# Attention with product-key experts on one core: three groups of tokens gathered and one dense, in place of two and two, with slots paced by counted VectorE work

## The chip, the core and the metric

One core of a Trainium2 chip runs the kernel. Its engines work in order, each from its own queue, and wait for each other by semaphores: TensorE (PE in the profile, PEld for its weight loads), VectorE (DVE), ScalarE (ACT), GpSimd (POOL, which here only starts gathers after the beginning) and SyncE (SP, which issues nearly all other transfers, in order). The metric is the device time of one execution in microseconds, the median of three runs.

## The reference, cut to what matters

```python
xn = layernorm(x)                       # x: 2048 tokens, 512 wide
out = x + A(xn) + B(xn)

# A: 32 query heads of 16, one key and one value head
p = softmax((xn @ wq) @ k.T * 16 ** -0.5);  A = (p @ v) @ wo

# B: 32 heads; per head two scores of 64 keys, the best two of each
s1, s2 = q1 @ k1.T, q2 @ k2.T           # q = xn @ w_q
cand = t1[:, None] + t2[None, :]        # 4 sums of the best 2 and 2
top_s, top_e = the best 2 of the 4      # top_e = i1 * 64 + i2, of 4096 experts
g = softmax(top_s)
act = gelu(xn . u[top_e])
B = sum over heads and the two of g * act * v[top_e]
```

So each token has 32 x 2 = 64 experts out of 4096, each a row of `u` (512) and a row of `v` (512).

## The kernel before

**Staging.** The 2048 tokens are 16 tiles of 128, in four groups of 512 (`GT` = 4 tiles). A prologue normalises and transposes the groups, projects queries, keys and values, and stores what is needed later in DRAM. Then a loop of 256 steps (and 24 more to run out) carries three streams, and its order of instructions on each engine is written out by hand (a manual schedule): what the program emits first, an engine does first.

- *Attention* (`att_steps`): 32 units (a block of 512 queries and four heads each) of 16 key tiles; a step does two key tiles. TensorE makes scores (L317), ScalarE exponentials (L320), TensorE the sums over values (L331). Behind each unit its sums are copied out (L339). From step 72 on, every 64 steps, `block_out` multiplies four tiles of a finished query block by `wo`.
- *Scores of the experts* (`score_thread`, a generator that gives the cost of each piece in units of about a microsecond of TensorE): for each chunk `c` of four heads (`NC` = 8) the weight is formed once (`wp_make`), for each tile of the group an `item` does twelve matmuls (L531) and VectorE finds the best of eight sets of 64 keys (L541, L543); after four tiles `batch` turns them into indices and gates. `run_scores` lets the thread run in each step until its spent cost reaches `aim`, which grows evenly to `FILL` at step 256.
- *The experts themselves*, in one of two ways. For a **gathered** group each of a token's 64 experts is a slot: GpSimd gathers the 128 rows of `uv` (1024 wide, 512 KB) for one tile (`gather`, L842), VectorE takes the product with the tokens (`dot`, L854), three small operations (`CHAIN`) and ScalarE's tanh (L870) give a weight for four slots at a time (`weigh`, L877), and VectorE adds the weighted row of `v` to the tile's total (`add`, L889). For a **dense** group (`dense`), 32 one-hot products (L713 to L716, L729) spread the gates over all 4096 experts into DRAM (`d_g`); then 32 blocks of 128 experts are computed whole: `pact` (L781), the activation on ScalarE and VectorE, and `pout` (L764), whose sums VectorE adds to the totals (L767). Rows of `ub` and `vb` are split in two parts by ScalarE (L677) and VectorE (L678).

**Order around the change.** In a step, `mid` emits the tanh of the groups of four that are complete, then this step's products (`todo` of them), then `go` emits adds, one at a time between the small operations and what is left of a dense block, and after them up to four gathers. At the step's end `fill` runs the score thread. A gather is emitted only while fewer than 12 (`NGB`) slots are between gather and add, and two fewer while `lent` is 2: `load_wo` borrows two of the gather buffers, from the step where `i` is 124 (modulo 128; `i` is twice the step) until 30, and near the end. Adds take slots whose tanh was emitted, so not before the step behind their product.

The products per step come from `pos`: 2.4 while group 0 is scored, then 1.9, 2.3 or 1.5 by what the thread does (`dense_on`), and in the last quarter evenly what is left. The groups are scored in the order of `SEQ`: 0, two chunks of 1, 2 (then its dense work), the rest of 1, 3 (then its dense work). Groups 0 and 1 are gathered (`NSP` = 2).

A tile's total holds the residual and the experts' part. The attention part is joined through DRAM: whichever of the two is ready first is stored to `d_part` and read back into `fin` when the other comes (`block_out`, `experts_out`, `load_fin`), and the sum is stored.

Of the kernel before, what the change touches and what calls it, by code (L numbers as in the profile page):

```python
# [10 lines left out]
F32 = mybir.dt.float32  # L11
# [11 lines left out]
P = 128  # L23
S = 2048
D = 512
# [27 lines left out]
@with_exitstack  # L53
def tile_kernel(ctx, tc, x, wq, wkv, wo, wqT, kT, uv, ub, vb, out):
    nc = tc.nc
    pool = lambda name, **kw: ctx.enter_context(tc.tile_pool(name=name, **kw))
    dram = pool("dram", bufs=1, space=DRAM)
    const = pool("const", bufs=1)
    big = pool("big", bufs=1)
    late = [None]  # L60
# [18 lines left out]
    d_part = [dram.tile([P, D], F32, name=f"dpart{t}") for t in range(NT)]  # L79


    ident = const.tile([P, P], F32, name="ident")
# [40 lines left out]
    XT, XN, ACC, XP = {}, {}, {}, [None]  # L123
# [256 lines left out]
        nc.vector.tensor_mul(on, OT.pop(pp), rs)  # L380
        ON[pp] = on

    DONE_A, DONE_B, OUTS = {}, {}, []
    WO, lent = [], [0]

    def load_wo():
# [25 lines left out]

    PL = []

    FIN = {}

    def load_fin(t):
        fin = late[0].tile([P, D], F32, name="fin", tag="fin", bufs=1)
        nc.sync.dma_start(fin, d_part[t])
        FIN[t] = fin  # L420

    def block_out(qb, j):
        t = 4 * qb + j
        p = xtile("pwo")
        for k in range(KC):
            nc.tensor.matmul(p, ON[4 * qb + k][:, j * P:(j + 1) * P], WO[k // 2][:, k % 2, :],  # L426
                             start=k == 0, stop=k == KC - 1)
        if t in FIN:
            fin = FIN.pop(t)

            def total():
                nc.vector.tensor_add(fin, fin, p)
                store(lambda: nc.sync.dma_start(out[t * P:(t + 1) * P, :], fin))

            behind(total)
        else:
            def keep():
                fin = late[0].tile([P, D], F32, name="fin", tag="fin", bufs=1)
                nc.scalar.copy(fin, p)
                store(lambda: nc.sync.dma_start(d_part[t], fin))  # L440

            on_act(keep)
        DONE_A[t] = True

    def experts_out(t):

        if t >= 12:
            return True
        if t in FIN:
            fin = FIN.pop(t)  # L450
            nc.vector.tensor_add(fin, fin, ACC[t])
            store(lambda: nc.sync.dma_start(out[t * P:(t + 1) * P, :], fin))
        elif t in DONE_A:
            load_fin(t)
            return False
        else:
            acc = ACC[t]
            store(lambda: nc.sync.dma_start(d_part[t], acc))
        DONE_B[t] = True
        return True  # L460


    WC = {}
# [12 lines left out]
    def wp_make(c):  # L476

        wt = [big.tile([P, 2, 512], F32, name="wt", tag="da", bufs=2) for _ in range(2)]
        for h in range(4):
            for n in range(4 * c + h + 1, min(4 * c + h + 3, 4 * NC) if late[0] else 4):  # L480
                if ("raw", n // 4, n % 4) not in WC:
                    wp_load(n // 4, n % 4)
            w = WC.pop(("raw", c, h))
            p = xtile("pw")
            for s in range(2):
                nc.tensor.matmul(p[s * E:(s + 1) * E, :], kTs[:, s, :], w[:, s, :], start=True, stop=True)
            nc.scalar.copy(wt[h // 2][:, h % 2, :], p)
            yield 0.9
        WC[c] = []
        for k in range(KC):  # L490
            p = xtile("pwt")
            for h in range(4):
                nc.tensor.transpose(p[:, h * P:(h + 1) * P], wt[h // 2][:, h % 2, k * P:(k + 1) * P], ident)
            wk = wk_tile()
            nc.vector.tensor_copy(wk[:, 0, :], p)
            nc.vector.tensor_tensor(out=wk[:, 1, :], in0=p, in1=wk[:, 0, :], op=OP.subtract)  # L496
            WC[c].append(wk)
            store(lambda k=k, wk=wk: nc.sync.dma_start(d_w[c][:, k], raw(wk[:])))
            yield 0.45

    def wp_read(n, ks=range(KC)):
        for k in ks:
# [1 line left out]
            nc.sync.dma_start(raw(wk[:]), d_w[SEQ[n][1]][:, k])  # L504
            WC.setdefault(n, []).append(wk)

    SEQ = ([(0, c) for c in range(NC)] + [(1, c) for c in range(2)] + [(2, c) for c in range(NC)]
           + [(1, c) for c in range(2, NC)] + [(3, c) for c in range(NC)])
    M8, I8 = {}, {}
    BT = 4  # L510

    def item(n_, ti):
        ph, c = SEQ[n_]
        nph, nc_ = SEQ[n_ + 1] if n_ + 1 < len(SEQ) else (None, None)
        t = TPH * ph + ti
# [24 lines left out]
        for s in range(8):  # L540
            nc.vector.max(m8[:, jb, s, :], p[:, s * E:(s + 1) * E])  # L541
# [102 lines left out]
    def dense(DG, after):  # L644
# [64 lines left out]
        def onehot(q):  # L709
            if q < NQ:  # L710
                tb = q * TB
                oa = kt(F16, (P, P, TB))
                nc.vector.tensor_tensor(out=oa, in0=io, in1=bc(0, tb, P), op=OP.is_equal)  # L713
                ob = kt(F16, (P, NB, TB))
                nc.vector.tensor_tensor(out=ob, in0=io[:, :NB, :], in1=bc(1, tb, NB), op=OP.is_equal)
                nc.vector.tensor_mul(ob, ob, bc(2, tb, NB))  # L716
                OH[q] = oa, ob

        onehot(0)
        onehot(1)  # L720
        for q in range(NQ):
# [5 lines left out]
            p = xtile("pg")  # L727
# [45 lines left out]
        for b in range(NB):  # L773
# [47 lines left out]
        yield from sums()  # L821
        if after is not None:
            wp_read(after, range(2, KC))
        OUTS.extend(range(GT * DG, GT * DG + GT))

# [5 lines left out]
    NSL = len(slots)  # L831
# [48 lines left out]
    def add(m):  # L880
        ph, c, ti, s = slots[m]
        n, i = divmod(m, SB)
        weigh(n)
        if i == SB - 1:
            weigh(n + 1)
        w = WT[n]
        acc = ACC[TPH * ph + ti]
        v = UV.pop(m)[:, D:]
        nc.vector.scalar_tensor_tensor(acc, v, w[:, i:i + 1], acc, op0=OP.mult, op1=OP.add)  # L889
        if c == NC - 1 and s == NEG - 1:  # L890
            OUTS.append(TPH * ph + ti)


    g_next, d_next, a_next, a_ready = [0], [0], [0], [0]
# [72 lines left out]
                yield from dense(ph, n + 1 if n + 1 < len(SEQ) else None)  # L967
                dense_on[0] = 0

    dense_on = [0]  # L970
    sgen = score_thread()
    spent = [0.0]

# [19 lines left out]
    def att_steps(d, mid, fill):  # L993
# [4 lines left out]
        if out_now and 4 * qb + j in DONE_B:  # L998
            load_fin(4 * qb + j)
        if i < STEPS:  # L1000
            u, kc = divmod(i, 16)
            if i == 0:
# [97 lines left out]
    with tc.manual_schedule(engines={E_.PE, E_.Activation, E_.DVE, E_.Pool, E_.SP}):  # L1100
        done0 = spent[0]
        half = STEPS // 2
        pos = 0.0
        for d in range(half + 24):


            if d < half * 3 // 4:
                pos += 2.4 if len(IDX) < NC * TPH else (1.9, 2.3, 1.5)[dense_on[0]]
            else:
                pos += max(0.0, NSL - pos) / max(half - 4 - d, 1)  # L1110

            todo = min(int(pos + 0.001), NSL) - d_next[0]

            def mid():
                post = POST[:]
# [51 lines left out]
        while a_next[0] < NSL:  # L1167
# [3 lines left out]
            adds(SB)  # L1171
            run(STORES)
            gathers(NGB)
        assert not OUTS
        run(STORES)


# [35 lines left out]
```

## Time and profile before

| | us |
|---|---|
| median of 3 runs (2034.71 to 2038.64) | 2036.56 |
| the profiled execution | 2035.25 |
| its span, first to last instruction | 2033.5 |
| TensorE busy in it | 1889.3 |
| VectorE busy | 1742.0 |
| ScalarE busy | 1245.1 |
| GpSimd busy | 585.9 |
| mean granted TensorE clock | 0.959 |

The profile is one execution. A group of instructions is named by engine and source line, with what it writes and reads; busy time is the union of its instructions, and instructions of one engine overlap at their ends, so the mean duration of one is longer than the distance from its start to the next one's. A wait is given to the instruction that ended it. Times in a timeline are microseconds from the span's start.

### The profile page before, as it was taken

What the parts mean: (1) busy time and instruction counts of PE and PEld (TensorE: products, weight loads), DVE (VectorE), ACT (ScalarE), POOL (GpSimd) and SP (SyncE); (2) the same over time, 40 slices, a digit from 0 to 9 for tenths busy, and PEclk for the clock granted to TensorE, in tenths of its full rate; (3) what the DMA queues carried; (4) which work ended last, traced back from release to release, by engine and by line L of the source; (5) the groups of instructions that cost most, each with busy time, mean ns of one, the idle gap of its engine ahead of it and who ended that gap; (6) DMA issues with size and microseconds to landing.
All of it is one profiled execution on the core that took longest, in us unless ns stands there. A gap on an engine that the chain in (4) does not pass through costs nothing.

```text
span 2033.5 us, 34691 instructions
## 1 busy us (share of the span) xinstructions
PE 1889.3 (93%) x10990; PEld 1006.7 (50%) x10990; DVE 1742.0 (86%) x6809; ACT 1245.1 (61%) x1710; POOL 585.9 (29%) x542
## 2 busy tenths in 40 slices
PE   6869989999988998899999999999979989999997
PEld 4634444455544453555555545554545435555553
DVE  7638898989998876889989779999999778999993
ACT  3236555555546787577767565555558747777773
POOL 2202233322222232334424332222223233333310
PEclk9989999999998898999999999999989889999998
DMA  7856788886764778677888878777558887778751
GB/s 273 303 190 216 274 286 292 315 312 231 259 222 116 214 226 263 215 245 237 264 269 279 309 264 284 285 239 239 184 175 233 264 272 242 251 236 264 234 193 63
DMA packets 239882, 494.79 MB, mean 243 GB/s; under 512 B 93380, under 2 KB 93380, under 8 KB 239692
## 3 DMA queue, kind: packets, MB, share of 16 engines
q0 software_dynamic: 73728, 268.47, 39.8%
q1 hardware_dynamic: 163960, 222.44, 33.4%
q10 hardware_dynamic: 2004, 1.61, 0.3%
q8 instruction: 88, 1.44, 0.3%
q14 instruction: 102, 0.84, 0.1%
HBM read 429.51 MB, written 57.64 MB: 240 GB/s over the span
## 4 chain that ended last, share of the span: by engine, by line
PE 56%; DVE 26%; DMA 5%; issue 3%; ACT 3%; SPq 1%; another core or an unknown queue 0%; ACTq 0%; DVEq 0%
PE pv L331 16%; PE sc L317 11%; PE psc L531 10%; PE pact L781 7%; PE pout L764 6%; DVE xa L889 5%; DVE i L543 4%; DVE g L854 4%; DVE m L541 3%; PE pwo L426 2%; PE pg L729 2%; ACT pt L320 2%; DMA gy<-dg 1%; DVE oh L713 1%; DVE wk L678 1%
## 5 line engine op out<-in xcount | busy, mean ns | idle before, releaser
L320 ACT ACTIVATE pt<-sc 128x1024 f32<-128x1024 f32 x1024 | 993.3, 1025 | 558.3 <-PE sc L317 520.1
L842 POOL DMA_INDIRECT g<-in_uv_dram,idx x512 | 569.1, 1111 | 1374.8 <-DVE xa L889 753.3
L331 PE MATMUL pv<-pt,vaug 128*32 128x512 f32 x4096 | 517.4, 624 | 0.0
L317 PE MATMUL sc<-qa,kaug 64*128 64x512 f32 x2048 | 394.0, 459 | 27.8 <-ACT pt L320 26.7
L531 PE MATMUL psc<-wk,xt 128*128 128x512 f32 x1536 | 384.8, 401 | 15.8 <-DVE wk L496 6.7
L889 DVE SCALAR_TENSOR_TENSOR xa<-g,w,xa 128x512 f32<-128x512 f32 x512 | 371.3, 749 | 0.0
L854 DVE CUSTOM_DVE_ANT_0 g<-g,xa 128x512 f32<-128x512 f32 x512 | 338.6, 686 | 0.0
L531 PEld LDWEIGHTS psc<-wk,xt 128*128 128x128 f32 x1536 | 282.3, 189 | 110.1 <-issue 32.4
L317 PEld LDWEIGHTS sc<-qa,kaug 64*128 64x128 f32 x2048 | 159.5, 189 | 352.4 <-ACT pt L320 222.2
L331 PEld LDWEIGHTS pv<-pt,vaug 128*32 128x32 f32 x4096 | 110.0, 112 | 261.9 <-issue 260.2
L764 PE MATMUL pout<-wk,wd 128*128 128x512 f32 x768 | 198.2, 406 | 10.6 <-DVE da L767 4.4
L543 DVE FIND_INDEX8 i<-m,psc 128x8 uint32<-128x64 f32 x1024 | 207.4, 229 | 0.0
L781 PE MATMUL pact<-xt,wk 128*128 128x512 f32 x768 | 197.1, 403 | 4.3 <-DVE da L767 4.3
L764 PEld LDWEIGHTS pout<-wk,wd 128*128 128x128 f32 x768 | 142.4, 190 | 58.8 <-DVE da L767 6.8
L781 PEld LDWEIGHTS pact<-xt,wk 128*128 128x128 f32 x768 | 140.8, 189 | 53.7 <-issue 17.9
L541 DVE MAX8 m<-psc 128x8 f32<-128x64 f32 x1024 | 146.7, 219 | 17.6 <-PE psc L531 15.3
L877 DVE SCALAR_TENSOR_TENSOR w<-gth,ga 128x4 f32<-128x4 f32 x128 | 20.7, 162 | 95.5 <-ACT gth L870 93.2
L767 DVE TENSOR_TENSOR da<-da,pout 128x512 f32<-128x512 f32 x128 | 82.9, 684 | 8.8 <-PE pout L764 8.7
L678 DVE TENSOR_TENSOR wk<-rw,wk 128x512 fp32r<-128x512 f32 x128 | 84.6, 688 | 3.9 <-ACT wk L677 3.9
L729 PE MATMUL pg<-oh 128*128 128x32 f16 x1024 | 73.7, 246 | 10.0 <-DVE oh L716 9.2
L713 DVE TENSOR_TENSOR oh<-oh 128x2048 f16<-128x2048 f16 x64 | 78.0, 1220 | 5.6 <-PE pg L729 5.6
L729 PEld LDWEIGHTS <-oh 128*128 128x128 f16 x1024 | 68.6, 164 | 21.8 <-issue 10.1
(151 smaller groups left out, 1373.8 us busy)
## 6 DMA issues: line engine op xcount, KB each, us to landing
wk<-dw SPq DMA_DIRECT2D x96, 512.0 KB
wqt<-in_wqT_dram SPq DMA_DIRECT2D x32, 512.0 KB
dw<-wk SPq DMA_DIRECT2D x32, 512.0 KB
rw<-in_ub_dram SPq DMA_DIRECT2D x64, 256.0 KB
rw<-in_vb_dram SPq DMA_DIRECT2D x64, 256.0 KB
dg<-gst SPq DMA_DIRECT2D x32, 512.0 KB
gy<-dg SPq DMA_DIRECT2D x64, 256.0 KB
qa<-dqh SPq DMA_DIRECT2D x128, 64.0 KB
```

The lines of the kernel that those rows point to most:

```text
L317: nc.tensor.matmul(p[:, b, :], kaug[o:o + 64, kc * P:(kc + 1) * P], QA[u][o:o + 64, i, :], start=True, stop=True)
L320: nc.scalar.activation(pt, p, AF.Exp, scale=SCALE)
L331: nc.tensor.matmul(PV[u][32 * j:32 * j + 32, :], vaug[:, kc, :], pt[:, b, :], start=kc == 0, stop=kc == 15)
L531: nc.tensor.matmul(p, XT[g][k][:, a, j * P:(j + 1) * P], WC[n_][k][:, bb, :], start=n == 0, stop=n == 11)
L541: nc.vector.max(m8[:, jb, s, :], p[:, s * E:(s + 1) * E])
L543: nc.vector.max_index(i8[:, jb, s, :], m8[:, jb, s, :], p[:, s * E:(s + 1) * E])
L729: nc.tensor.matmul(p[:, i * NB:(i + 1) * NB], oa[:, :, i], ob[:, :, i], start=True, stop=True)
L764: nc.tensor.matmul(p, wd[:, a, j * P:(j + 1) * P], vs[:, c, :], start=n == 0, stop=n == 5)
L781: nc.tensor.matmul(p, us[:, a, k * P:(k + 1) * P], XT[DG][k][:, c, :], start=n == 0, stop=n == 11)
L842: nc.gpsimd.indirect_dma_start(out=gt, out_offset=None, in_=uv, in_offset=bass.IndirectOffsetOnAxis(ap=IDX[ph, c, ti][:, s:s + 1], axis=0))
L854: nc.vector.tensor_tensor_reduce(u, u, XN[TPH * ph + ti], scale=1.0, scalar=0.0, op0=OP.mult, op1=OP.add, accum_out=a[:, i:i + 1])
L889: nc.vector.scalar_tensor_tensor(acc, v, w[:, i:i + 1], acc, op0=OP.mult, op1=OP.add)
```

## The change

Groups 0, 1 and 2 are gathered (768 slots in place of 512) and group 3 alone is dense, so groups are scored in their order. The buffers of indices and gates grow from 9 to 17 batches. `FILL` is lowered from 948 to 704, as the thread has one dense group less. The step's number of products no longer follows fixed rates: a counter `vec` adds a cost for each piece of VectorE's other work as it is emitted, and each step the products may take what is left of an even share of the whole; they never pass the gathers that are emitted. The first copy in `wp_make` moves from VectorE to ScalarE. `block_out` adds the attention part straight into the tile's total on VectorE, and the experts' last add stores the total; `d_part`, `fin` and the branches for either order are gone.

```diff
-NSP = 2
+NSP = 3
-NIDX = 9
+NIDX = 17
-FILL = 948.0
+FILL = 704.0
+V_ITEM, V_BATCH, V_SUB, V_OH, V_BLOCK, V_SLOT = 2.64, 3.0, 0.7, 1.97, 5.45, 1.35
+OH_PART = 0.82
...
     def block_out(qb, j):
...
-        if t in FIN:
-            fin = FIN.pop(t)
-
-            def total():
-                nc.vector.tensor_add(fin, fin, p)
-                store(lambda: nc.sync.dma_start(out[t * P:(t + 1) * P, :], fin))
-
-            behind(total)
-        else:
-            def keep():
-                fin = late[0].tile([P, D], F32, name="fin", tag="fin", bufs=1)
-                nc.scalar.copy(fin, p)
-                store(lambda: nc.sync.dma_start(d_part[t], fin))
-
-            on_act(keep)
-        DONE_A[t] = True
+        acc = ACC[t]
+        behind(lambda: nc.vector.tensor_add(acc, acc, p))
+        DONE_A.add(t)
 
     def experts_out(t):
...
+        assert t in DONE_A
+        acc = ACC.pop(t)
+        store(lambda: nc.sync.dma_start(out[t * P:(t + 1) * P, :], acc))
...
-            nc.vector.tensor_copy(wk[:, 0, :], p)
+            nc.scalar.copy(wk[:, 0, :], p)
             nc.vector.tensor_tensor(out=wk[:, 1, :], in0=p, in1=wk[:, 0, :], op=OP.subtract)
+            vec[0] += V_SUB
...
-    SEQ = ([(0, c) for c in range(NC)] + [(1, c) for c in range(2)] + [(2, c) for c in range(NC)]
-           + [(1, c) for c in range(2, NC)] + [(3, c) for c in range(NC)])
+    SEQ = [(ph, c) for ph in range(NPH) for c in range(NC)]
...
+        vec[0] += V_ITEM
         if jb == BT - 1:
             batch(ph, c, b)
+            vec[0] += V_BATCH
...
+                vec[0] += V_OH
...
+            vec[0] += V_BLOCK
...
         if c == NC - 1 and s == NEG - 1:
-            OUTS.append(TPH * ph + ti)
+            experts_out(TPH * ph + ti)
...
+        others = (NPH * NC * (TPH * V_ITEM + V_BATCH) + NC * KC * V_SUB + 512 // 16 * V_OH + NB * V_BLOCK)
+        mean = (others - vec[0] + NSL * V_SLOT) / (half - 4 - (1 - OH_PART) * 24 * (NPH - NSP))
+        room = vec[0]
         for d in range(half + 24):
-
-
-            if d < half * 3 // 4:
-                pos += 2.4 if len(IDX) < NC * TPH else (1.9, 2.3, 1.5)[dense_on[0]]
-            else:
-                pos += max(0.0, NSL - pos) / max(half - 4 - d, 1)
-
-            todo = min(int(pos + 0.001), NSL) - d_next[0]
+            room += mean * (OH_PART if dense_on[0] == 2 else 1)
+            pos = max(pos, min(pos + 4.0, (room - vec[0]) / V_SLOT, NSL) if d < half - 4 else NSL)
+            todo = min(int(pos + 0.001), NSL, g_next[0]) - d_next[0]
...
-                    if OUTS and (2 * d < 140 or (2 * d - 140) % 128 >= 24) and experts_out(OUTS[0]):
-                        OUTS.pop(0)
```

More of the change, by code (lines that the diff above doesn't have):

```diff
@@ L78, in tile_kernel @@
     d_inv = dram.tile([15, 8, 512], F32, name="dinv")
-    d_part = [dram.tile([P, D], F32, name=f"dpart{t}") for t in range(NT)]
     ident = const.tile([P, P], F32, name="ident")
@@ L381, in pair_tail @@
         ON[pp] = on
-    DONE_A, DONE_B, OUTS = {}, {}, []
+    DONE_A = set()
     WO, lent = [], [0]
@@ L413, in tile_kernel @@
     PL = []
-    FIN = {}
-    def load_fin(t):
-        fin = late[0].tile([P, D], F32, name="fin", tag="fin", bufs=1)
-        nc.sync.dma_start(fin, d_part[t])
-        FIN[t] = fin
     def block_out(qb, j):
@@ L427, in block_out @@
                              start=k == 0, stop=k == KC - 1)
-        if t in FIN:
-            fin = FIN.pop(t)
-            def total():
-                nc.vector.tensor_add(fin, fin, p)
-                store(lambda: nc.sync.dma_start(out[t * P:(t + 1) * P, :], fin))
-            behind(total)
-        else:
-            def keep():
-                fin = late[0].tile([P, D], F32, name="fin", tag="fin", bufs=1)
-                nc.scalar.copy(fin, p)
-                store(lambda: nc.sync.dma_start(d_part[t], fin))
-            on_act(keep)
-        DONE_A[t] = True
-    def experts_out(t):
[L447 to L455, printed above, removed]
-        else:
[L457 to L460, printed above, removed]
+        acc = ACC[t]
+        behind(lambda: nc.vector.tensor_add(acc, acc, p))
+        DONE_A.add(t)
+    def experts_out(t):
+        assert t in DONE_A
+        acc = ACC.pop(t)
+        store(lambda: nc.sync.dma_start(out[t * P:(t + 1) * P, :], acc))
     WC = {}
@@ L823, in dense @@
             wp_read(after, range(2, KC))
-        OUTS.extend(range(GT * DG, GT * DG + GT))
+        assert DG == NPH - 1
     slots = [(ph, c, ti + i, 2 * h + k) for ph in range(NSP) for c in range(NC) for ti in range(0, TPH, 2)
@@ L968, in score_thread @@
                 dense_on[0] = 0
-    dense_on = [0]
+    dense_on, vec = [0], [0.0]
     sgen = score_thread()
@@ L997, in att_steps @@
         qb, j = (i - 144) // 128, (i - 144) % 128 // 4
-        if out_now and 4 * qb + j in DONE_B:
-            load_fin(4 * qb + j)
         if i < STEPS:
@@ L1103, in tile_kernel @@
         pos = 0.0
+        others = (NPH * NC * (TPH * V_ITEM + V_BATCH) + NC * KC * V_SUB + 512 // 16 * V_OH + NB * V_BLOCK)
+        mean = (others - vec[0] + NSL * V_SLOT) / (half - 4 - (1 - OH_PART) * 24 * (NPH - NSP))
+        room = vec[0]
         for d in range(half + 24):
-            if d < half * 3 // 4:
-                pos += 2.4 if len(IDX) < NC * TPH else (1.9, 2.3, 1.5)[dense_on[0]]
-            else:
-                pos += max(0.0, NSL - pos) / max(half - 4 - d, 1)
-            todo = min(int(pos + 0.001), NSL) - d_next[0]
+            room += mean * (OH_PART if dense_on[0] == 2 else 1)
+            pos = max(pos, min(pos + 4.0, (room - vec[0]) / V_SLOT, NSL) if d < half - 4 else NSL)
+            todo = min(int(pos + 0.001), NSL, g_next[0]) - d_next[0]
             def mid():
@@ L1173, in tile_kernel @@
             gathers(NGB)
-        assert not OUTS
         run(STORES)
```

## The prediction

> **What bounds the kernel now.** I read the page's busy shares first, then the same shares by stage.
>
> ```profile
> span 2033.5 us, 34691 instructions
> PE 1889.3 (93%) x10990; PEld 1006.7 (50%) x10990; DVE 1742.0 (86%) x6809; ACT 1245.1 (61%) x1710; POOL 585.9 (29%) x542
> ```
> ```profile
> 0.00:148.60 148.60, 108.11 (x461) 68.62 (x461) 83.11 (x260) 41.40 (x74) 25.32 (x40) 0.93 0.71 256
> 2011.90:2033.50 21.60, 10.78 (x20) 3.67 (x18) 7.28 (x12) 0.80 (x2) 0.00 (x0) 0.74 0.38 122
> ...
> 1210.70:1266.50 55.80, 55.80 (x320) 31.13 (x318) 54.84 (x357) 32.11 (x39) 14.09 (x15) 1.00 0.86 295
> ...
> 1507.00:1605.00 98.00, 94.94 (x850) 49.36 (x850) 95.50 (x204) 79.82 (x133) 33.91 (x27) 0.90 0.85 230
> 1605.00:2011.90 406.90, 394.87 (x2172) 208.07 (x2172) 338.03 (x748) 285.57 (x388) 120.71 (x106) 0.98 0.70 228
> sum 1863.30, PE 1770.46 PEld 934.45 DVE 1651.66 ACT 1202.94 POOL 560.54; mean PE 354.09 PEld 186.89 DVE 330.33 ACT 240.59 POOL 112.11
> ```
> The second view has, after the stretch and its length, the busy time of PE, PEld, DVE, ACT and POOL, the granted clock and the DMA share. Rows one and two are the start and the tail, the others lie in the loop of 256 steps, whose five stages sum to 1863.3 us, 7.3 us a step. TensorE bounds the last dense stage (394.9 of 406.9 us busy). In a score stretch (1210.7 to 1266.5) both TensorE (all of it) and VectorE (98%) are full, and in the one-hot stage VectorE is (97%). So the kernel is bound by TensorE with VectorE close behind, and VectorE can be held at 97 to 98% while its data is there. Is it there? VectorE's waits say so:
>
> ```profile
> DVE w L877 <- ACT gth L870: 93.2, 49, 8.5
> ...
> DVE gy L802 <- DMA gy<-dg: 18.0, 5, 11.1
> ```
> (us in total, times, longest.) No row names a gather: in this kernel no product (L854) ever waited for its rows of `uv`.
>
> **The change part by part: engines.** One dense group goes. Rows of the groups (busy us, mean ns of one):
>
> ```profile
> L764 PE MATMUL pout<-wk,wd 128*128 128x512 f32 x768 | 198.2, 406 | 10.6 <-DVE da L767 4.4
> L781 PE MATMUL pact<-xt,wk 128*128 128x512 f32 x768 | 197.1, 403 | 4.3 <-DVE da L767 4.3
> L729 PE MATMUL pg<-oh 128*128 128x32 f16 x1024 | 73.7, 246 | 10.0 <-DVE oh L716 9.2
> L678 DVE TENSOR_TENSOR wk<-rw,wk 128x512 fp32r<-128x512 f32 x128 | 84.6, 688 | 3.9 <-ACT wk L677 3.9
> L713 DVE TENSOR_TENSOR oh<-oh 128x2048 f16<-128x2048 f16 x64 | 78.0, 1220 | 5.6 <-PE pg L729 5.6
> L715 DVE TENSOR_TENSOR oh<-oh 128x512 f16<-128x512 f16 x64 | 26.8, 419 | 0.0
> L716 DVE TENSOR_TENSOR oh<-oh 128x512 f16<-128x512 f16 x64 | 27.2, 425 | 6.4 <-ACT oh L704 4.3
> L495 DVE CAST wk<-pwt 128x512 fp32r<-128x512 f32 x32 | 21.8, 683 | 18.0 <-PE pwt L493 18.0
> ```
> TensorE loses half of the first three, 99 + 99 + 37 = 235 us, and falls to some 1655. VectorE's instructions overlap at their ends, so I take them from start to start, in a stretch where it stands still nowhere:
>
> ```profile
> 306.33 1.15 DVE L541 MAX8 m<-psc 128x8 f32<-128x64 f32 x8
> ...
> 308.98 0.68 DVE L854 CUSTOM_DVE_ANT_0 g<-g,xa 128x512 f32<-128x512 f32 x1
> ...
> 309.57 0.69 DVE L854 CUSTOM_DVE_ANT_0 g<-g,xa 128x512 f32<-128x512 f32 x1
> ...
> 310.19 0.75 DVE L889 SCALAR_TENSOR_TENSOR xa<-g,w,xa 128x512 f32<-128x512 f32 x1
> 310.85 0.16 DVE L863 SCALAR_TENSOR_TENSOR gq<-act 128x4 f32<-128x4 f32 x1
> 310.92 0.75 DVE L889 SCALAR_TENSOR_TENSOR xa<-g,w,xa 128x512 f32<-128x512 f32 x1
> ```
> A score item takes 308.98 - 306.33 = 2.65 us, a product 0.61, an add 0.66 (310.85 - 310.19), a small one 0.07 (310.92 - 310.85). A slot (product, add, four small ones per four slots) is 1.35 or a little over; I take 1.36. A dense block has nine 512-element instructions (two L678, two L767, five of the activation) at some 0.61, 5.5 us; a one-hot is 1.22 + 0.42 + 0.43 less three overlaps, 1.9. VectorE loses 32 x (5.5 + 1.9) = 237, and 32 casts (L495) at 0.61, 20; it gains 256 slots x 1.36 = 348. That is +91: 1833 us.
>
> The casts go to ScalarE, busy 61%; if it were full they would cost 19. The attention part's add replaces an add at L432 or L451, one for one, and its round trip through DRAM goes: 0. The store of a finished tile is new ahead of the next group's loads on SP's queue, and behind them stand the next unit's queries and score weights; the slowest store of this kind in the chain is
>
> ```profile
> 1659.29 6.68 DMA out_dram<-fin
> ```
> so 0 to 7 us for each of four pairs of tiles. A new tile's first gather stands several slots ahead of its product, so I take 0. More index buffers cost nothing on any engine.
>
> Without a new wait, then: 1833, the idle time of VectorE in the start (148.6 - 83.1 = 65) and the tail (21.6 - 7.3 = 14), and 22 of small waits in the loop (the one-hot stage's row has 2.6% idle, 45 of 1740; I take half, since TensorE now runs ahead). That is 1934, 100 us under the span.
>
> **The change part by part: the gathers' notice.** A gather can be issued once an earlier slot's add has freed one of 12 buffers, of which 2 are lent to `wo` for 17 steps in every 64. The loop fixes in which step each gather, product and add stands, from counts and constants alone, so it can be counted through. For the kernel before this gives 19, 19, 19, 19, 16, 15, 15, 15, 12, 12, 12 products in the first eleven eights of steps; the trace agrees (each row counts two instructions a product):
>
> ```profile
> 202.40:269.50 67.10, 12.49 (x38) 0.96 0.82 279
> 394.50:452.80 58.30, 10.66 (x32) 1.00 0.91 322
> ...
> 691.60:740.80 49.20, 8.09 (x24) 0.97 0.72 205
> ```
> There the product stands two to five steps behind its gather; only two slots, at the very start, have one step. For the changed loop the count gives 27, 28, 25, 23, 27, 25, 21, 23, then 29 in steps 72 to 79, 31 in 136 to 143, and 26, 31, 29 in 200 to 223. Of 768 products 256 stand one step behind their gather, in 103 of the 256 steps; in 51 of these steps three or four of them. In steps 75 to 83 all four products of each step are rows asked for in the step before.
>
> What such a step costs hangs on how long a gather takes. POOL's rows and the packets of its queue (one gather is 144) counted up to a time tell:
>
> ```profile
> 999.26 1.21 POOL L842 DMA_INDIRECT g<-in_uv_dram,idx  x1 [5.27 <-DVE xa L889]
> 1000.77 0.94 POOL L842 DMA_INDIRECT g<-in_uv_dram,idx  x1 [0.30 <-issue]
> 1002.02 0.94 POOL L842 DMA_INDIRECT g<-in_uv_dram,idx  x1 [0.30 <-issue]
> 1003.69 1.21 POOL L842 DMA_INDIRECT g<-in_uv_dram,idx  x1 [0.74 <-DVE xa L889]
> ...
> q0 software_dynamic: 564, 2.08, 66.0%
> q0 software_dynamic: 576, 2.10, 61.6%
> ...
> 1961.34 1.13 POOL L842 DMA_INDIRECT g<-in_uv_dram,idx  x1 [4.82 <-DVE gq L863]
> ...
> q0 software_dynamic: 120, 0.48, 44.8%
> q0 software_dynamic: 144, 0.52, 42.6%
> ```
> The two counts of the burst reach from 1000 to 1009.9 and to 1010.7: the last of four lands 6.2 to 7.0 us after POOL took it. Those of the last gather, alone, reach from 1961.3 to 1965.2 and 1965.7: some 4.4. POOL starts one every 1.25 us, 0.3 behind the add. I take 6.0, near the burst, because the short-notice gathers come in bursts, and keep 4.4 and 7.0.
>
> A step of four: products end at 2.5, the adds at 3.3, 4.0, 4.8, 5.5; POOL starts at 3.6, 4.8, 6.1, 7.3; the last lands at 13.3, and its product stands 1.9 behind the next step's beginning. The step cannot be shorter than 11.4 us, where VectorE has 5.5 us of work: 5.9 short, 3.2 with a score item in the step. VectorE works in order, so adds, small operations and score items queue behind the waiting product; TensorE's `x` banks wait for those, and the next gathers for the adds. Summing this subtraction over the steps as counted, each with its own products, adds and other work, gives 171 for the 51 steps with three or four and 75 for the rest: 246 us. At 4.4 it is 131, at 7.0 341.
>
> [...]
>
> The sum: 1934 + 246 = 2180, and the 1.75 us that the profiled execution (2035.25) has beside its span, 2182; that execution is 1.3 us under the median of the runs, so 2185.
>
> **Rivals.** (a) *The short-notice gathers land before VectorE comes to them.* Faster if the stalls sum to less than 99 us (2033.5 - 1934), which the count reaches at a landing of some 3.7 us. For it: nothing waits for a gather today, and a VectorE held up elsewhere gives each gather time. Against it: even the lone gather takes 4.4. Time: stalls of 40 to 80, 1995. [...]
>
> (b) *The DMA engines fill up and gathers take 8 us.* The gathers' queue today:
>
> ```profile
> q0 software_dynamic: 73728, 268.47, 39.8%
> q1 hardware_dynamic: 163960, 222.44, 33.4%
> ```
> Half as many gathers again make 59.7% of the old span; with some 28% left on the other queue the engines are at 88%, near the 86 to 91% that single stretches show today. Stalls of 440: 2375. Against it: stalls stretch the time over which the bytes are spread.
>
> (c) *TensorE or a waiting queue still sets the loop*, and the gain from the dense group is just given back: 2035. Against it: 1655 us of TensorE's work leaves 200 idle.
>
> (d) *The pacing leaves slots to the end*, so that the tail grows: the count has 762 of 768 products done by step 252, so I give it nothing.
>
> **How the numbers follow.** Forecast 0.67: 2185, with its own range 2070 to 2280 from stalls of 131 to 341. (a) 0.18, (b) 0.10, (c) 0.05. The range 2010 to 2300 takes in the likeliest case and the upper part of (a), and leaves out the rest of (a) and most of (b). Faster by over 0.2% (4 us, about what a measurement of this kernel can tell from none): 0.18; within it 0.05, from (c); slower 0.77.
>
> **What would show it.** Right: a row of VectorE's waits that names L854 and a gather's DMA, or an unexplained stand before L854, some 250 us in all; most of it near the 17 steps of the loans and in the dense stage after; some 30 products in an eight of steps of 80 us or more; TensorE near 75%, VectorE's busy time near 1833. Wrong at the sum: that busy time off by over 20. Wrong at the notice: no wait at L854, and VectorE at 96% of the loop, as in (a); or waits at L854 of twice the size with gathers of 8 us and more, as in (b). Stands before L541 or L877 instead would say (c).

## The result and the profile after

| | before | after |
|---|---|---|
| median | 2036.03 us (4 runs) | 2210.70 us (4 runs, 2204.55 to 2213.06) |
| ratio after to before, 95% interval | | 1.085 (1.083 to 1.088) |
| span of the profiled execution | 2033.5 us | 2209.6 us |
| TensorE busy | 1889.3 (93%) | 1809.9 (82%) |
| VectorE busy | 1742.0 (86%) | 1820.4 (82%) |
| mean granted TensorE clock | 0.959 | 0.901 |

The change makes the kernel 8.5% slower: 174.7 us, where 148 had been predicted. In the new source the product stands at L829 (L854 before), the add at L864 (L889), the gather at L817 (L842), the scores at L319 (L317), the sums over values at L333 (L331). The page's busy line, and VectorE's waits (us in total, times, longest):

```profile
span 2209.6 us, 32881 instructions
PE 1809.9 (82%) x9698; PEld 858.9 (39%) x9698; DVE 1820.4 (82%) x7337; ACT 1181.0 (53%) x1603; POOL 865.7 (39%) x797
```
```profile
DVE g L829 <- DMA g<-in_uv_dram,idx: 257.6, 159, 4.9
DVE qt L231 <- ACT qt L230: 17.2, 6, 5.6
DVE wk L467 <- ACT wk L466: 16.8, 6, 15.4
DVE rsb L407 <- DMA ot<-e: 12.5, 1, 12.5
DVE w L852 <- ACT gth L845: 8.5, 9, 2.5
```
The first row did not exist before: the products wait for their rows 159 times, 257.6 us in all. The next three lie in the start and the tail. The last row was the largest of before, 93.2 us for the gate's tanh; now the tanh is nearly always early, and not only because VectorE is held up elsewhere: the row stays small (16.7 us) in the run without gathers below, where no product waits for its rows. TensorE and VectorE are both at 82%, so neither is busy enough to be the bound; they wait for a chain that goes back and forth. The page's chain says which:

```profile
DVE 11%; DMA 9%; issue 3%; PE 3%; POOL 2%; ACT 0%; ACTq 0%; SPq 0%; DVEq 0%; POOLq 0%
DMA g<-in_uv_dram,idx 9%; DVE xa L864 4%; DVE g L829 3%; POOL g L817 2%; PE pv L333 1%; DVE wk L651 1%; DVE da L741 1%; PE sc L319 1%; PE pout L738 1%; DVE gy L779 1%; DVE wd L778 1%; DVE gy L775 0%; PE pact L755 0%; DVE gy L776 0%; PE pwl L401 0%
```
The followed part is short, but its members are a ring: the gather's DMA, the product, the add that frees the buffer, and POOL, which asks for the next rows. One turn of it, near 780 us, first POOL's timeline, then VectorE's (start, length):

```profile
777.55 0.94 POOL L817 DMA_INDIRECT g<-in_uv_dram,idx  x1 [4.80 <-DVE gq L838]
778.88 1.29 POOL L817 DMA_INDIRECT g<-in_uv_dram,idx  x1 [0.40 <-DVE gy L839]
```
```profile
777.86 0.75 DVE L864 SCALAR_TENSOR_TENSOR xa<-g,w,xa 128x512 f32<-128x512 f32 x1
...
780.62 0.68 DVE L829 CUSTOM_DVE_ANT_0 g<-g,xa 128x512 f32<-128x512 f32 x1
...
783.43 0.69 DVE L829 CUSTOM_DVE_ANT_0 g<-g,xa 128x512 f32<-128x512 f32 x1 [2.12 <-DMA g<-in_uv_dram,idx]
...
785.46 0.69 DVE L829 CUSTOM_DVE_ANT_0 g<-g,xa 128x512 f32<-128x512 f32 x1 [1.33 <-DMA g<-in_uv_dram,idx]
```
Counted from the start, the gather at 777.55 is the 252nd and the product at 783.43 the 252nd too: 5.9 us from POOL's start to the product, and 6.6 for the next pair. VectorE stands 2.12 and 1.33 us in between. Over the 157 products that stood more than 0.3 us the median of this distance is 6.3 us.

Where the stands lie, in the changed kernel's windows (start and end, length, busy time of PE, PEld, DVE, ACT and POOL, granted clock, DMA share, GB/s):

```profile
691.90:769.70 77.80, 58.24 (x257) 21.77 (x256) 54.09 (x223) 32.30 (x42) 29.96 (x28) 0.87 0.67 223
...
846.00:905.00 59.00, 52.77 (x302) 25.61 (x302) 57.27 (x331) 34.01 (x43) 23.98 (x24) 0.94 0.81 283
1196.20:1274.10 77.90, 58.14 (x254) 21.92 (x254) 55.85 (x228) 32.13 (x42) 28.79 (x28) 0.85 0.66 218
...
1760.70:1847.70 87.00, 60.91 (x287) 28.30 (x287) 62.52 (x154) 40.53 (x57) 37.13 (x32) 0.82 0.71 230
1847.70:1938.90 91.20, 61.56 (x284) 28.92 (x282) 62.81 (x157) 40.54 (x58) 37.64 (x31) 0.79 0.68 221
```
Rows one and three are steps 72 to 79 and 136 to 143, the last two steps 208 to 223; they hold 30 to 32 products each and take 78 to 91 us, with VectorE busy 69 to 72% and the DMA engines two thirds: nobody is full. Row two is an eight with fewer products, where VectorE is at 97%. Cut by window, the waits for gathers sum to 40.3 us in steps 72 to 87, 31.4 in 136 to 151 and 77.1 in 200 to 223, so 149 of the 257.6 us in 56 of 256 steps; 51.8 more lie in the first 72.

### The profile page after: what moved, and what is told of

Read it like the earlier page. It is cut to its first block, busy times and chain, and to the rows that moved or that the text cites. A ratio compares the mean times of both kernels' runs of the same rounds, so it can differ in the third digit from the quotient of the medians.

```text
span 2209.6 us, 32881 instructions
## 1 busy us (share of the span) xinstructions
PE 1809.9 (82%) x9698; PEld 858.9 (39%) x9698; DVE 1820.4 (82%) x7337; ACT 1181.0 (53%) x1603; POOL 865.7 (39%) x797
## 3 DMA queue, kind: packets, MB, share of 16 engines
q0 software_dynamic: 110592, 402.70, 53.8%
q1 hardware_dynamic: 114232, 182.58, 24.5%
## 5 line engine op out<-in xcount | busy, mean ns | idle before, releaser
L817 POOL DMA_INDIRECT g<-in_uv_dram,idx x768 | 850.7, 1108 | 1303.5 <-DVE gq L838 643.3
L829 DVE CUSTOM_DVE_ANT_0 g<-g,xa 128x512 f32<-128x512 f32 x768 | 504.0, 685 | 259.5 <-DMA g<-in_uv_dram,idx 257.6
L319 PE MATMUL sc<-qa,kaug 64*128 64x512 f32 x2048 | 444.0, 492 | 239.8 <-ACT pt L322 218.0
L333 PE MATMUL pv<-pt,vaug 128*32 128x512 f32 x4096 | 578.7, 689 | 0.0
L864 DVE SCALAR_TENSOR_TENSOR xa<-g,w,xa 128x512 f32<-128x512 f32 x768 | 562.1, 746 | 0.0
L319 PEld LDWEIGHTS sc<-qa,kaug 64*128 64x128 f32 x2048 | 178.2, 200 | 634.1 <-ACT pt L322 435.4
L333 PEld LDWEIGHTS pv<-pt,vaug 128*32 128x32 f32 x4096 | 117.4, 120 | 288.1 <-issue 286.4
L738 PE MATMUL pout<-wk,wd 128*128 128x512 f32 x384 | 109.8, 432 | 33.5 <-DVE gy L776 28.0
L755 PE MATMUL pact<-xt,wk 128*128 128x512 f32 x384 | 102.2, 410 | 6.9 <-DVE wk L651 5.9
L738 PEld LDWEIGHTS pout<-wk,wd 128*128 128x128 f32 x384 | 74.7, 202 | 63.8 <-DVE gy L776 31.1
L755 PEld LDWEIGHTS pact<-xt,wk 128*128 128x128 f32 x384 | 70.4, 192 | 36.0 <-issue 13.0
L514 DVE MATCH_VALUE_LOAD i<-m,psc 128x8 f32 x1024 | 72.8, 71 | 0.1
L829 DVE DVE_READ_ACCUMULATOR2_ANT act<- 128x1 f32 x768 | 63.0, 82 | 0.0
```

Source lines behind the costliest of these rows:

```text
L319: nc.tensor.matmul(p[:, b, :], kaug[o:o + 64, kc * P:(kc + 1) * P], QA[u][o:o + 64, i, :], start=True, stop=True)
L333: nc.tensor.matmul(PV[u][32 * j:32 * j + 32, :], vaug[:, kc, :], pt[:, b, :], start=kc == 0, stop=kc == 15)
L738: nc.tensor.matmul(p, wd[:, a, j * P:(j + 1) * P], vs[:, c, :], start=n == 0, stop=n == 5)
L755: nc.tensor.matmul(p, us[:, a, k * P:(k + 1) * P], XT[DG][k][:, c, :], start=n == 0, stop=n == 11)
L817: nc.gpsimd.indirect_dma_start(out=gt, out_offset=None, in_=uv, in_offset=bass.IndirectOffsetOnAxis(ap=IDX[ph, c, ti][:, s:s + 1], axis=0))
L829: nc.vector.tensor_tensor_reduce(u, u, XN[TPH * ph + ti], scale=1.0, scalar=0.0, op0=OP.mult, op1=OP.add, accum_out=a[:, i:i + 1])
```

## The experiments

Theory: VectorE waits for gathers that are asked for one step before their product. Rivals: the DMA engines are too full; or the loss is TensorE's or the pacing's own, and the waits only fill time that would be lost anyway. All edits are to the changed kernel; ratios are to the kernel before, with 95% intervals.

**No gathers, and gathers that nobody reads.** The first edit keeps only the first ten gathers and reuses their buffers; the product reads the other half of the rows, so that it doesn't overwrite what is reused.

```diff
+        if m >= 10:
+            UV[m] = HELD[m % 10]
+            return
...
-        nc.vector.tensor_tensor_reduce(u, u, XN[TPH * ph + ti], ...
+        nc.vector.tensor_tensor_reduce(u, UV[m][:, D:], XN[TPH * ph + ti], ...
```


> Only the first ten gathers are made; every later product and add uses these ten buffers again, in the same order of instructions, so the experts' part is computed from the wrong rows. Theory A (short-notice gathers hold VectorE): the 258 us that VectorE stood before L829 in the changed kernel go and nothing takes their place, so the time is 2211 - 258 = 1953, between 1935 and 1975, with VectorE's busy time unchanged near 1820. Rival B (the added 256 slots make VectorE's work itself, with the order of work around it, too long): the waits are a symptom, and the time stays above 2100.

1945.04 us, ratio 0.954 (0.950 to 0.958).

```profile
span 1945.0 us, 31305 instructions
PE 1729.2 (89%) x9698; PEld 837.2 (43%) x9698; DVE 1803.2 (93%) x7337; ACT 1179.0 (61%) x1603; POOL 25.6 (1%) x39
```
VectorE's work is the same in kind and number (7337 instructions) and it is busy 93%. The rest of the change is thus worth a gain of 4.6%; everything beyond that comes with the gathers, by traffic or by waiting.

The second edit was to part these two: all gathers are made, and products and adds use the first six buffers (the product again reads the other half of the rows).

```diff
+        if m < 6:
+            HELD[m] = gt
-        UV[m] = gt
+        UV[m] = HELD[m % 6]
```


> All 768 gathers are made and move their 402.7 MB, but products and adds read the first six buffers again, so that nobody waits for the other gathers (the experts' part is computed from the wrong rows). Theory A (notice): within 20 us of the kernel without gathers, about 1955 to 1975. Rival C (the DMA engines are too full, so that gathers and the loads beside them are slow): most of the loss stays, above 2100, with waits on other transfers; a half-way 2030 would give both a share.

2335.13 us, far above the theory's 1955 to 1975, and above the 2100 that the rival of full engines named. POOL's waits tell what held the gathers:

```profile
POOL g L818 <- PE pwo L421: 620.4, 3, 355.1
POOL g L818 <- DMA g<-in_uv_dram,idx: 324.9, 271, 5.6
```
With no add behind them the gathers were bound to other things: to the end of the loan (`pwo`, once for 355 us) and to the gather that had the buffer before. Between these waits they ran ahead of the loop: a gather starts 27 to 431 us before its slot's product, where in the changed kernel the median is 11 us. After the second loan they came as one burst, and a window over it (columns as above, then the DMA queues with packets, MB and share of the engines) shows the loop standing:

```profile
1326.00:1510.00 184.00, 33.82 (x130) 17.04 (x126) 37.78 (x180) 13.84 (x17) 127.95 (x133) 0.58 0.99 381
```
```profile
q0 software_dynamic: 19086, 69.50, 98.3%
q1 hardware_dynamic: 519, 0.56, 1.0%
```
The gathers' queue has 98.3% of the DMA engines, and TensorE is busy 34 of 184 us; what its long stands (up to 45 us) waited for, the profile doesn't name, so what ties them to the burst is not shown. The jam is the edit's own, since the two large queues of the changed kernel take 53.8 and 24.5%; so the edit doesn't part waiting from traffic at the changed kernel's pace. The next one keeps the waits of POOL as they are.

**The rows of the slot four before.** The product waits for, and reads, the first half of the rows that came four slots earlier; gathers, buffers, adds and order are those of the changed kernel.

```diff
-        u = UV[m][:, :D]
+        u = UV.get(m - 4, UV[m])[:, :D]
```


> Order, buffers and all 768 gathers as in the changed kernel; only the product of a slot reads the rows of the slot four before, where these are still held (so the experts' part is computed from the wrong rows), and its add reads its own. A product's rows were then asked for about one step earlier, at the same traffic. Theory A (notice): the waits before the products fall from 258 to some 20 us and the time to 1945 + 20 = 1965, at most 1990. Rival C (gathers and the loads beside them slow each other on the DMA engines): the waits go elsewhere and the time stays above 2080.

1973.13 us, 0.969 (0.964 to 0.974). VectorE's wait for gathers and the gathers' queue on the page:

```profile
DVE g L829 <- DMA g<-in_uv_dram,idx: 7.3, 7, 2.0
```
```profile
q0 software_dynamic: 110592, 402.70, 59.2%
```
All 402.70 MB were moved, in a shorter time than in the changed kernel, and the kernel was 3% faster than before. So the gathers' traffic, with what is left of waiting, costs 28 us (1973 against 1945) and the notice 238 (2210.7 - 1973.1). At this pace of gathers that rules out the full DMA engines, and TensorE's bound too.

**One buffer less.**

```diff
-NGB = 12
+NGB = 11
```


> One gather buffer is taken away (11 in place of 12), nothing else; the loop counted through again has 378 products at one step's notice and 382 us of stalls, 136 more. Theory A: 2347, between 2310 and 2370. Rivals B and C (work, traffic): within 20 us of 2211.

2346.19 us, 1.152 (1.146 to 1.158).

```profile
DVE g L829 <- DMA g<-in_uv_dram,idx: 387.0, 250, 5.9
```
One buffer takes 135 us, of which the waits for gathers explain 129 (387.0 - 257.6). The count, which says how many products stand one step behind their gather, had named this time to a microsecond. That close a hit is luck: in three of the experiments below the same count is off by 19 us (the loans), 12 (16 buffers) and 21 (even pacing). What it gets right is the direction and the rough size.

**No loans before slot 550.** The first two loads of `wo` go into tiles of `wqt`, idle by then, and the gathers keep all 12 buffers.

```diff
-            w = gtile(F32, (P, 2, D), "wo")
+            w = (big.tile([P, 2, D], F32, name="wo", tag="wqt", bufs=2) if g_next[0] < 550
+                 else gtile(F32, (P, 2, D), "wo"))
...
-            lent[0] = 2
+            lent[0] = 2 if i > 300 else 0
```


> The first two of the four times that attention's output weights are loaded they go into two tiles that are idle then, so that no gather buffers are lent in steps 62 to 79 and 126 to 143. Theory A: counted through, 41 us of stalls go (29 to 14 and 31 to 14 in the two eights of steps with the most products, a little around them): 2170, between 2155 and 2190. If the number of buffers had no part in it (B, C): 2211.

2189.06 us, 1.074 (1.071 to 1.077): -21.6, half of what was expected.

```profile
DVE g L830 <- DMA g<-in_uv_dram,idx: 234.8, 139, 5.1
```
The waits for gathers fell by 22.8 (257.6 to 234.8). Steps 72 to 79 went from 78 to 63 us, 136 to 143 from 78 to 67; the others hardly moved. The reason for the half lies in the changed kernel's own trace. Products, adds and gathers up to a time, in views of lines cut by window, POOL's up to 772.5 us and VectorE's up to 776.2:

```profile
L817 POOL DMA_INDIRECT g<-in_uv_dram,idx x251 | 265.4, 1057 | 491.4 <-DVE gq L838 249.1 <-DVE xa L864 62.9 <-DVE e L569 56.9
```
```profile
L864 DVE SCALAR_TENSOR_TENSOR xa<-g,w,xa 128x512 f32<-128x512 f32 x239 | 174.7, 746 | 0.0
```
That is step 79, still inside the loan as the count had it, and yet the gathers are 12 ahead of the adds and not 10. `lent` holds back only the place of a gather in POOL's program. POOL itself waits for its buffer's last user, and with 12 buffers in rotation that is the add 12 slots before, unless `wo` stood in the rotation between them. In the changed kernel's trace no gather begins before the add 12 slots back is over, but of the 183 gathers that the program emits during loans 107 begin before the add ten slots back is over. The loan was counted as if it cost two buffers for 17 steps; the first loan does so for about eight of them (gathers of steps 70 to 77).

**Four more buffers while the dense stage's tiles are idle.** Up to step 144 gathers may also take four tiles of `wd`, except for a group's first 32 slots; and no loan before slot 550, as above.

```diff
+        if inside["g"] < NGB - lent[0]:
+            gt, KIND[m] = gtile(), "g"
+        else:
+            gt, KIND[m] = late[0].tile([P, 2 * D], F32, name="g", tag="wd", bufs=4), "wd"
...
-        while ... g_next[0] < a_next[0] + NGB - lent[0] and most > 0:
+        while ... g_next[0] < a_next[0] + NGB - lent[0] + extra[0] * (g_next[0] % 256 >= 32) and most > 0:
...
+            extra[0] = 4 if d < 145 else 0
```


> Until step 144 four more gather buffers are used (tiles that the dense stage needs later), except for the first 32 slots of a group, and the first two loads of the output weights take idle tiles, so that nothing is lent before step 241 modulo the third load at step 190. The order of products and adds is as in the changed kernel. Theory A: counted through, the 106 us of stalls before step 150 go and the 140 in the dense stage stay: 2105, between 2085 and 2135 (the run without the first two loans gave half of what was counted, which would make it the upper end). Rivals B and C: within 20 us of 2211.

2092.70 us, 1.028 (1.023 to 1.034).

```profile
DVE g L835 <- DMA g<-in_uv_dram,idx: 131.9, 81, 5.0
```
Room for gathers is all that changed, and 118 us come back, of which the loans alone gave 22 above.

**Adds ahead of products.** Outside the one-hot stage a step's adds are emitted first, so that they, and the gathers behind them, don't queue behind a product that waits.

```diff
+                sums = min(a_ready[0] - a_next[0], max(todo, 3) if d < half else 4)
+                if dense_on[0] != 2:
+                    while rest or sums > 0:
+                        if sums > 0:
+                            adds(1)
+                            sums -= 1
+                        if rest:
+                            rest.pop(0)()
                 dots(d_next[0] + todo - 1)
```


> The changed kernel whole, with one thing moved: outside the one-hot stage a step's adds are emitted ahead of its products, not behind them, so that a buffer is freed at the beginning of a step and its gather has the rest of the step besides. Theory A: counted through as in the prediction at 6.0 us a gather, the stalls fall from 246 to 12 us, so the time falls by some 235 to 1975, between 1950 and 2010, which is also under the kernel before (2036). Rivals B and C: same work, same bytes, so no change beyond 20 us from 2211; or slower, if VectorE now waits for ScalarE's tanh at the step's start (L852), at most 256 steps x 1 us.

2061.37 us, 1.012 (1.008 to 1.015); 86 us above the expectation. VectorE's waits:

```profile
DVE w L852 <- ACT gth L845: 47.5, 42, 4.7
DVE g L829 <- DMA g<-in_uv_dram,idx: 26.7, 17, 4.2
```
The wait for gathers did fall as expected, by 231 us, but the time by 149 only. A new wait came: the gate's tanh needs the small operations that stand behind the last products, and with the adds gone ahead nothing long stands between tanh and weight (47.5 against 8.5 us). VectorE's busy time also rose from 1820.4 to 1839.2; why, no run shows.

**Slots paced by the step number.** The count of VectorE's work is left out; the products are spread evenly.

```diff
-            room += mean * (OH_PART if dense_on[0] == 2 else 1)
-            pos = max(pos, min(pos + 4.0, (room - vec[0]) / V_SLOT, NSL) if d < half - 4 else NSL)
+            pos = min(NSL, NSL * (d + 1) / (half - 4))
```


> The counted pacing alone is taken out: the products follow an even 768/252 = 3.05 a step. Theory A: counted through, 148 products in place of 256 stand one step behind their gather and the stalls fall from 246 to 173 us, so the time falls by about 73 to 2138, between 2110 and 2165. Rival D (the counted pacing is what keeps VectorE evenly loaded, and without it steps full of score items and products run over): slower than 2211.

2116.89 us, 1.041 (1.036 to 1.045).

```profile
DVE g L829 <- DMA g<-in_uv_dram,idx: 143.0, 106, 4.1
```
The wait for gathers is 143.0 us in place of 257.6. So the counted pacing, as it stands in the change, costs 94 us: it puts four products into each step where VectorE has little else, and 12 buffers can't feed that.

**A version that beats both.** The 16 early buffers, and adds first only in steps in which some product's gather was emitted one step before.

```diff
+                if dense_on[0] != 2 and any(STEP[m] >= d - 1 for m in range(d_next[0], d_next[0] + todo)):
+                    while rest or sums > 0:
```


> The changed kernel with four more gather buffers where the dense weights' tiles stand idle and no early loans (as in e8), and with a step's additions ahead of its products only in the steps in which some product's gather was emitted one step before. Theory (a gather needs about one step more than the short-notice steps give it; the rest of the loss is a wait that the order of the additions moves): the count leaves 20 us of waits for gathers and 56 such steps; 1945 (no waits, e1) + 20 + 20 for the gate's tanh and the chain's small operations coming late behind the products (0.35 us a step, from e3's 47.5 over all steps) + 18 of unevenness = about 2000, range 1980 to 2030, under the kernel before. Rival (the loss is TensorE's and the pacing's, not the gathers' notice): it stays near e8, 2093, or near e3, 2061.

1996.24 us, ratio 0.979 (0.976 to 0.983): 2% faster than the kernel before, as expected. The waits, and the steps 72 to 79 and 208 to 223 of this version's windows:

```profile
DVE g L837 <- DMA g<-in_uv_dram,idx: 23.7, 16, 5.3
DVE w L860 <- ACT gth L853: 17.7, 23, 2.6
```
```profile
651.90:707.40 55.50, 51.21 (x260) 20.18 (x264) 53.88 (x227) 32.28 (x42) 29.35 (x27) 0.94 0.89 308
...
1619.30:1680.80 61.50, 53.80 (x285) 25.89 (x285) 59.12 (x149) 40.01 (x57) 35.47 (x31) 0.94 0.95 326
1680.80:1745.70 64.90, 54.26 (x282) 26.41 (x282) 62.73 (x159) 40.30 (x59) 36.48 (x32) 0.92 0.90 308
```
Against the rows of the changed kernel, the same work takes 55.5 in place of 77.8 us, 61.5 in place of 87.0, 64.9 in place of 91.2; VectorE's and POOL's busy times are about the same, the idle time is gone.

The same version, paced by the step number:

> As e9, with the slots paced by the step number (the rule of the kernel before stretched over the group) in place of VectorE's counted load. Theory: 16 us of waits left and 33 steps with the additions first, so about 1990, range 1975 to 2025, if the stages bear an uneven VectorE load per step; if the counted pacing is worth what it was made for once the gathers are in time, e10 is slower than e9 by 10 us or more.

2021.99 us, 0.992 (0.988 to 0.995). It is 26 us slower than with the counted pacing, and the second half of the expectation holds: once the gathers are mostly in time, pacing by counted work pays. Some of the 26 is again waiting for gathers (33.4 us against 23.7); which part of the rest is VectorE's uneven load was not tested. The same edit that gains 94 us in the changed kernel costs 26 here.

**The cast back on VectorE.**

```diff
-            nc.scalar.copy(wk[:, 0, :], p)
+            nc.vector.tensor_copy(wk[:, 0, :], p)
```


> The changed kernel with the two halves of the query's weights cast on VectorE again, as in the kernel before. If VectorE's own queue sets these stretches, its 20 us come back: 2231, range 2215 to 2245. If they fall into VectorE's idle time (it has some 130 us of it beside the waits for gathers), 2211 as without.

2210.76 us, against 2210.70: no difference. VectorE's busy time went from 1820.4 to 1839.4 and its wait for gathers from 257.6 to 244.3. What VectorE has more to do, it waits less: in these stretches the ring of gathers sets the time, and 19 us of VectorE's work are free.

## Why the prediction was right, point by point

It was right in sign, mechanism and place, and 26 us low. The profiled span against the sum of 2180:

| term | predicted | in the trace |
|---|---|---|
| VectorE busy | 1833 | 1820.4 |
| wait for gathers | 246 | 257.6 |
| idle in start and tail | 79 | 82 (68.7 + 12.8) |
| other idle time in the loop | 22 | 50 |
| span | 2180 | 2209.6 |

Start and tail are from the windows of the changed kernel:

```profile
0.00:147.90 147.90, 110.64 (x461) 69.78 (x461) 79.24 (x256) 45.95 (x81) 25.08 (x40) 0.93 0.73 263
2189.70:2209.60 19.90, 8.90 (x20) 3.13 (x18) 7.10 (x12) 0.58 (x1) 0.00 (x0) 0.83 0.38 119
```
The other idle time is what is left: 2209.6 - 1820.4 - 257.6 - 81.5.

- *The engines.* VectorE's +91 was +78. The step that failed most is the smallest term, the 22 us of small waits "in the loop": halved "since TensorE now runs ahead". They came to 50, more than the 45 that were halved. Rows of waits inside the loop make 30 of them (the tanh's 8.5 the largest; `qt`, `wk` and `rsb` of the rows above lie in the start and the tail), the rest are gaps too short for a row. TensorE was late in few of these (4.7 us), so its lead could take little away. Without gathers the same rest is already there: 1945.0 - 1803.2 = 142 us of idle time, some 63 of it inside the loop. The sum without a new wait, 1934, is near that run's span of 1945.0, and 34 under the 1968.4 of the run that moves all gathers and hardly waits for them.
- *The landing time.* 6.0 us was taken between 4.4 and 7.0; the products that waited show a median of 6.3. No product that waited more than 0.3 us came less than 4.2 us behind its gather (128 rows, beside other traffic), so none of these landed in the 3.7 us at which the prediction's count has the stalls at 99 us. The spread is wide: a tenth of the products that waited came 8.9 us or more behind their gather.
- *The loans.* Their place was right and their size about twice too large: 22 us of an expected 41, because `lent` moves an instruction in POOL's program and not what POOL waits for. So some of the 246 came from the wrong place, and the total is partly luck: the count had 106 us before step 150 and 140 behind it (the expectation of the 16 buffers says so), the trace has 133 in the first 152 steps and 124 behind them.
- *The casts.* The sum credits their move with 20 us. It is worth nothing while the waits stand (2210.76 against 2210.70).
- *TensorE.* "falls to some 1655", "TensorE near 75%": it fell to 1809.9, 82%. The removed work was counted right, within 16 us; what remained grew. Rows of before and then of after:

```profile
L331 PE MATMUL pv<-pt,vaug 128*32 128x512 f32 x4096 | 517.4, 624 | 0.0
L317 PE MATMUL sc<-qa,kaug 64*128 64x512 f32 x2048 | 394.0, 459 | 27.8 <-ACT pt L320 26.7 <-issue 0.3
```
```profile
L333 PE MATMUL pv<-pt,vaug 128*32 128x512 f32 x4096 | 578.7, 689 | 0.0
L319 PE MATMUL sc<-qa,kaug 64*128 64x512 f32 x2048 | 444.0, 492 | 239.8 <-ACT pt L322 218.0 <-ACT gth L845 10.6 <-issue 6.4
...
L738 PE MATMUL pout<-wk,wd 128*128 128x512 f32 x384 | 109.8, 432 | 33.5 <-DVE gy L776 28.0 <-DVE da L741 3.3 <-issue 2.3
L755 PE MATMUL pact<-xt,wk 128*128 128x512 f32 x384 | 102.2, 410 | 6.9 <-DVE wk L651 5.9 <-DVE da L741 1.0
...
L703 PE MATMUL pg<-oh 128*128 128x32 f16 x512 | 37.7, 246 | 6.9 <-DVE oh L689 6.1 <-ACT gst L708 0.7
```
  `pout`, `pact` and `pg` lost 88, 95 and 36, 219 of the 235 expected; `sc` and `pv`, whose number is the same, took 50 and 61 more. That didn't matter for the time, since TensorE was far from the bound, as the prediction had it.
- *The rivals.* (a), the gathers land in time, needed stalls under 99 us and put them, by the author's estimate, at 40 to 80; they were 257.6. (b), full engines, foresaw 8 us a gather; the two large queues use 78% of the engines' time in the changed kernel (53.8 + 24.5). (c), TensorE, is excluded by the runs of 1945 and 1973. (d) cost nothing: the last add ends at 2182 us, before the loop does (2188).

```profile
q0 software_dynamic: 110592, 402.70, 53.8%
q1 hardware_dynamic: 114232, 182.58, 24.5%
```
- *What would show it.* The wait at L829 with a gather's DMA came, 257.6 for "some 250 us in all", mostly where it was said. The eights "of 80 us or more" were 78, 78, 87 and 91.

The addition of attention's part in place, the larger index buffers and the new store were costed at nothing or nearly; none was tried alone. All of them are in the runs of 1945 and 1996 us, so together they can't cost much. Whether the gathers' notice in steps 208 to 223 can be bought without a new wait stays open: the versions with more room had none there, and only the order of the adds helped.

## What to carry to other kernels

Where a buffer is freed by the consumer's own last operation, the number of buffers is a rate: 12 slots over a ring of product, tanh, add, POOL and some 6 us of landing (a median of 6.3 for the products that waited); one buffer less cost 135 us here. Count how many steps lie between request and use at the new rate before trading work onto that ring; an engine at 82% can be the one that waits (VectorE here, 257.6 us for gathers). Pacing that fills an idle engine with the work that needs the ring makes things worse until the ring has the room (the counted pacing cost 94 us with 12 buffers and the old order, and gained 26 with room). And an order in the program is not a wait on the chip (107 of the 183 gathers emitted during loans began before the add ten slots back was over): look for what an engine's instruction really waits for.

## What the hardware showed unexpectedly

The granted clock of TensorE, on one core, was lower in the runs below in which TensorE was busy for a smaller share of the span. With the same 9698 matmuls it was 0.945 without gathers, 0.938 in the version that beats both, 0.901 in the changed kernel and 0.880 with 11 buffers, where TensorE was busy 89, 87, 82 and 79% of the span; the kernel before, with 10990 matmuls, had 0.959 at 93%. Within the changed kernel it is 0.94 in the even eight of the windows above (TensorE busy 52.77 of 59.00 us) and 0.79 in the last of them (61.56 of 91.20). Not every stage fits: the one-hot stage of the kernel before had 0.90 with TensorE busy 94.94 of 98.00 us. What sets the clock, no run here shows. Some matmuls of the same shape took longer in the changed kernel, `pv` 689 in place of 624 ns, while the experts' scores `psc` hardly did (403 and 401), and with the same 9698 matmuls TensorE's busy time was 1729 us without gathers and 1849 with 11 buffers: a busy share is no measure of work done here. What part of the longer `pv` is clock, and what part is modelled ends, no run here parts.
